# The pair of token blocks: products that pile up in one PSUM bank, weight sums on GpSimd, weight splits one f-tile ahead

## The chip, the cores and the metric

The kernel runs on one core of a Trainium2 chip. The metric is the device time of one execution in microseconds (us). The kernel before took 931.39 to 933.38 us in three runs, median 931.68.

Engines are named as the profile names them: PE is TensorE (its matmuls), PEld its weight loads, DVE is VectorE, ACT is ScalarE, POOL is GpSimd, SP issues DMAs. PSUM has eight banks, of which one 128x384 or 128x512 fp32 tile fills one. In the names of the profile "arena" and "arena_r" are the two views of the kernel's large SBUF buffer (float32 and fp32r), "ov_..." are buffers that take turns in one SBUF region, "banks" is PSUM, and "x2d" is a scratch tensor in DRAM.

## The reference

Three layers, one after the other, over 2304 tokens (4 batches of 576) of width 512:

```
x = linear attention(q, k, v)                      # features exp(+-(x@w_phi - max)), 8 heads of 64
g = x @ moe_w_gate                                 # 512 -> 1536
y = (g * sigmoid(g) * (x @ moe_w_val)) @ moe_w_out # 1536 -> 512
e = argmax(y @ moe2_w_gate)                        # 8 experts, one per token
out = prob[e] * sigmoid((y @ moe2_w_output_gate)[e]) * (relu(y @ w1[e]) @ w2[e])
```

The change lies in the second layer, the gated feed-forward.

## The kernel before, in words

Every fp32 product of the feed-forward is made of three fp32r matmuls: an operand is split in a high part (an ACT copy that rounds to fp32r, L549) and a low part (what is left, a subtraction on POOL, L552), and high·high, high·low and low·high are added up in PSUM. A weight tile is 128x512 for a block alone.

The tokens are cut in six blocks of 384 (n = 0 to 5), the width 1536 in twelve f-tiles of 128. Blocks 0 to 3 go one by one: for each f the gate product, the value product, the gate in between, and the output product of the f-tile before (`mm_o`). Blocks 4 and 5 go together, as "the pair" (L670). There the four products of a 2x2 block matrix are made of seven half products (Strassen and Winograd): A11, A12 and A22 are blocks of the weights, S1 to S4 sums of blocks, and the other operand is a block of x or one of the sums that `x_sums` has made of it (L638). In the order of the code a half product is six matmuls of 128x384 (L665 to L667), an output product nine of 128x512 (L619 to L621). So an f-tile of the pair has 42 + 9 matmuls on PE.

Each half product's weights are 256 wide and pass through a ring of 2048 columns (`ring`, `ahead`): as soon as a product is issued, what now has room is split. Before the first piece of an f-tile, `sums` makes the four weight sums on DVE (L558 to L561).

The products A11 to A22 of an f-tile land in four banks BA, BB, BX, BY. What they give is joined on DVE, ACT and POOL through SBUF: u2 is A11 (an ACT copy, L679) plus S2; z is S1 (ACT, L683) plus S3 (ACT, L686; the addition is on POOL); GP is the gate of A11+A12 (tanh L689, L690); gb is the gate of u2 plus S4 (L694, L695); va is GP times (u2 plus A22), which is split by L699 and one more addition for block 4's output product; and HB5, kept for later, is gb times (u2 plus z). The additions all go through `add` (L673), and its `eng` says where.

`rest` (L1226) puts in the output product of f-1 at the end of an f-tile, and steps of the third layer's routing (`fill`) in between: short DVE, ACT and PE work on the tokens that are ready. After the pair, the output product of block 4's last f-tile, its transposes and writes to x2d follow, and then block 5's twelve output products (L1247), each of HB5 split by `h5`. The first expert weights (`load_w`, `mw`) are fetched meanwhile.

The order on each engine is that of the program as a scheduler has sorted it per engine; what an instruction waits for are the tiles that it reads and writes, and each engine takes its instructions in order.

Of the kernel before, what the change touches and what calls it, by code (L numbers as in the profile page):

```python
# [23 lines left out]
NFT = DFF // P  # L24
# [157 lines left out]
def kernel(ctx, tc, qT, kT, v1, wphi, w1cat, wlog, mw1, mw2, consts, out):  # L182
# [334 lines left out]
    PRODS = ("A11", "S2", "S1", "S3", "A12", "S4", "A22")  # L517
    for f in range(NFT):
        uses += [(4, f, w) for w in PRODS] + [(4, f - 1, 2) if f else (3, NFT - 1, 2)]
    uses.append((4, NFT - 1, 2))  # L520
    uses += [(5, f, 2) for f in range(NFT)]
    where = {u: i for i, u in enumerate(uses)}
    ring, at_ = [], 0
    for u in uses:
        w = 512 if u[2] in (0, 1, 2) else 256
        if at_ % 2048 + w > 2048:
            at_ += 2048 - at_ % 2048
        ring.append((at_, w))
        at_ += w

    def wh(i):
        o, w = ring[i]
        return AR[:, 9216 + o % 2048:9216 + o % 2048 + w]

    def wl(i):
        o, w = ring[i]
        return AR[:, 11264 + o % 2048:11264 + o % 2048 + w]

    def source(i):
        n, f, w = uses[i]  # L540
        if w in (0, 1, 2):
            return WR[f][w]
        if w[0] == "A":
            o = 256 * (int(w[2]) - 1)
            return WR[f][int(w[1]) - 1][:, o:o + 256]
        return SS[f % 2][int(w[1]) - 1]

    def split_hi(i):
        ACT.activation(wh(i), source(i), AF.Copy)  # L549

    def split_lo(i):
        POOL.tensor_tensor(out=wl(i), in0=source(i), in1=wh(i).bitcast(F32), op=ALU.subtract)  # L552

    def sums(f):
        g0, g1 = WR[f][0][:, 0:256], WR[f][0][:, 256:512]
        v0, v1 = WR[f][1][:, 0:256], WR[f][1][:, 256:512]
        s1, s2, s3, s4 = SS[f % 2]
        DVE.tensor_tensor(out=s1, in0=v0, in1=v1, op=ALU.add)  # L558
        DVE.tensor_tensor(out=s2, in0=s1, in1=g0, op=ALU.subtract)
        DVE.tensor_tensor(out=s3, in0=g0, in1=v0, op=ALU.subtract)  # L560
        DVE.tensor_tensor(out=s4, in0=g1, in1=s2, op=ALU.subtract)  # L561

    def ahead(i):
        j = state["split"]
        while j < len(uses) and ring[j][0] + ring[j][1] - ring[i][0] <= 2048:
            if uses[j][2] == "A11":
                sums(uses[j][1])
            split_hi(j)
            split_lo(j)
            j += 1  # L570
# [748 lines left out]
```

## Time and profile before

| what | value |
|---|---|
| median of three runs | 931.68 us |
| the profiled execution | 931.75 us, of which 930.0 is the span on the core |
| PE busy | 888.2 us (96%) |
| DVE, ACT, POOL busy | 650.9, 573.3, 425.9 us (70, 62, 46%) |
| the pair, 490.3 to 622 us | 131.7 us, granted clock 0.99 |
| block 5's output products | to about 660 us |

A busy share is of the span. Matmuls are pipelined: each row gives a modelled duration of 0.33 us for a 128x384 matmul, but the next one starts earlier than that, so what a stretch costs PE is read from one start to the next, and a wait from a start that comes late. The granted clock is 1.00 where the engine runs at 2.4 GHz, and about 0.5 where it runs at 1.2 GHz. Rows of waits say which instruction of which line an engine stood idle for.

### The profile page before, as it was taken

The page shows a single profiled execution, that of the slowest core. Times are in us where ns is not written, and L with a number is a line of the kernel's source. Part 1 is how long each engine was busy: PE and PEld are TensorE (multiplying, and loading weights), DVE is VectorE, ACT ScalarE, POOL GpSimd, SP SyncE. Part 2 cuts the span into 40 slices and gives each one's busy share as a digit, 9 for nine tenths or more (in the row PEclk, how much of TensorE's full clock was granted, in tenths as well). Part 3 has the DMA queues.
Part 4 walks back from the last instruction along what each step waited for, and adds up shares of the span by engine and source line. Part 5 has one row for each costly group of instructions (what it writes and reads, how often), then busy time and mean ns, then how long its engine had stood idle before and what let it go on. Part 6 is the DMA issues. An engine that isn't in the chain of part 4 may idle for free. (4 is left out here: it accounts for less than half of the span.)

```text
span 930.0 us, 18143 instructions
## 1 busy us (share of the span) xinstructions
PE 888.2 (96%) x6979; PEld 769.6 (83%) x6979; DVE 650.9 (70%) x1075; ACT 573.3 (62%) x1051; POOL 425.9 (46%) x371
## 2 busy tenths in 40 slices
PE   8899999999999999999999988888999999999995
PEld 6789999999988899888888878776787888888884
DVE  6998785444337334554666889755799988899984
ACT  6877776444454444444545454445488988988883
POOL 1668988455543343335376676675104111222200
PEclk9999999999999999999999999998999999999998
DMA  8867542200111011200000000008401147156150
GB/s 242 222 179 205 188 141 63 75 1 1 27 50 27 15 41 29 72 16 1 2 1 35 1 1 2 1 11 314 151 24 35 47 132 279 71 186 260 44 191 9
DMA packets 20940, 78.88 MB, mean 85 GB/s; under 512 B 5359, under 2 KB 5615, under 8 KB 19057
## 3 DMA queue, kind: packets, MB, share of 16 engines
q1 hardware_dynamic: 17280, 67.60, 22.7%
q0 software_dynamic: 3200, 9.48, 3.1%
q8 instruction: 56, 0.92, 0.4%
q10 hardware_dynamic: 368, 0.60, 0.2%
q14 instruction: 36, 0.29, 0.1%
HBM read 123.24 MB, written 10.00 MB: 143 GB/s over the span
## 5 line engine op out<-in xcount | busy, mean ns | idle before, releaser
L552 POOL TENSOR_TENSOR arena_r<-arena,arena_r 128x512 fp32r<-128x512 f32 (+1 forms) x252 | 287.7, 1155 | 236.0 <-ACT arena_r L549 232.6
L549 ACT ACTIVATE arena_r<-arena 128x512 fp32r<-128x512 f32 (+1 forms) x252 | 137.7, 556 | 160.1 <-PE banks L581 94.0
L1052 DVE TENSOR_TENSOR arena_r<-arena,arena_r 128x1024 fp32r<-128x1024 f32 x160 | 188.0, 1224 | 20.7 <-ACT arena_r L1049 19.8
L1049 ACT ACTIVATE arena_r<-arena 128x1024 fp32r<-128x1024 f32 x160 | 161.2, 1066 | 15.9 <-PE banks L1088 10.2
L580 PE MATMUL banks<-arena_r 128*128 128x384 f32 x384 | 135.3, 352 | 2.3 <-DVE arena L592 1.7
L582 PE MATMUL banks<-arena_r 128*128 128x384 f32 x384 | 129.0, 336 | 0.0
L581 PE MATMUL banks<-arena_r 128*128 128x384 f32 x384 | 128.9, 336 | 0.0
L1088 PE MATMUL banks<-arena_r 128*128 128x512 f32 x480 | 116.2, 396 | 0.1
L1116 POOL DMA_INDIRECT out_dram<-arena x20 | 21.7, 1084 | 203.0 <-ACT arena L1115 202.7
L1088 PEld LDWEIGHTS banks<-arena_r 128*128 128x128 f32 x480 | 88.3, 188 | 19.9 <-ACT arena_r L1080 1.7
L619 PE MATMUL banks<-arena_r 128*128 128x512 f32 x216 | 88.1, 408 | 3.6 <-ACT arena_r L699 3.6
L621 PE MATMUL banks<-arena_r 128*128 128x512 f32 x216 | 86.5, 403 | 1.1 <-DVE arena_r L673 1.1
L620 PE MATMUL banks<-arena_r 128*128 128x512 f32 x216 | 86.3, 399 | 0.0
L580 PEld LDWEIGHTS banks<-arena_r 128*128 128x128 f32 x384 | 72.1, 188 | 7.8 <-DVE arena L592 2.1
L592 DVE SCALAR_TENSOR_TENSOR arena<-arena,banks 128x384 f32<-128x384 f32 x48 | 26.5, 551 | 70.7 <-ACT arena L589 70.7
L581 PEld LDWEIGHTS banks<-arena_r 128*128 128x128 f32 x384 | 72.3, 188 | 0.6
L582 PEld LDWEIGHTS banks<-arena_r 128*128 128x128 f32 x384 | 72.1, 188 | 0.0
L1110 PE MATMUL banks<-arena_r 128*128 128x512 f32 x160 | 62.6, 391 | 1.0 <-ACT arena_r L1049 0.7
L1112 PE MATMUL banks<-arena_r 128*128 128x512 f32 x160 | 62.6, 391 | 0.0
L1111 PE MATMUL banks<-arena_r 128*128 128x512 f32 x160 | 62.5, 390 | 0.0
L320 DVE TENSOR_REDUCE arena<-banks 128x6 f32<-128x768 f32 x48 | 45.8, 954 | 22.4 <-PE banks L312 21.5
L312 PEld LDWEIGHTS banks<-arena 64*128 64x128 f32 x576 | 39.5, 187 | 17.2 <-issue 7.1
(160 smaller groups left out, 1745.1 us busy)
## 6 DMA issues: line engine op xcount, KB each, us to landing
arena<-mw SPq DMA_DIRECT2D x40, 2048.0 KB
ov_conv<-w1cat SPq DMA_DIRECT2D x24, 512.0 KB
arena<-w1cat SPq DMA_DIRECT2D x12, 512.0 KB
arena<-v SPq DMA_DIRECT2D x16, 325.0 KB
x2d<-arena SPq DMA_DIRECT2D x18, 256.0 KB
arena<-qT SPq DMA_DIRECT2D x15, 288.0 KB
arena<-kT SPq DMA_DIRECT2D x15, 288.0 KB
arena<-consts ACTq DMA_DIRECT2D x1, 327.5 KB
```

Source lines behind the costliest of these rows:

```text
L549: ACT.activation(wh(i), source(i), AF.Copy)
L552: POOL.tensor_tensor(out=wl(i), in0=source(i), in1=wh(i).bitcast(F32), op=ALU.subtract)
L580: PE.matmul(ps, w_h[:, c], xh, start=(k == 0), stop=False)
L581: PE.matmul(ps, w_h[:, c], xl, start=False, stop=False)
L582: state["pe"] = PE.matmul(ps, w_l[:, c], xh, start=False, stop=(k == 3)).ins
L619: PE.matmul(ps, gh[:, ts_], woh, start=(f == 0), stop=False)
L620: PE.matmul(ps, gh[:, ts_], wol, start=False, stop=False)
L621: PE.matmul(ps, gl[:, ts_], woh, start=False, stop=(f == NFT - 1))
L1049: a = ACT.activation(h, src, AF.Copy)
L1052: DVE.tensor_tensor(out=l, in0=src, in1=h.bitcast(F32), op=ALU.subtract)
L1088: PE.matmul(PS[:, HB[h], :], lhs, w[:, h * 512:(h + 1) * 512], start=a, stop=b)
L1110: PE.matmul(ps, HTH[:, k, :], wh[:, cs], start=(k == 0), stop=False)
```

## The change

All 12 f-tiles of the pair are written anew:

- A11, S2, S1 and S4 are added up in one bank `bb` (bank 3 or 6 in turn), and ACT copies what stands there three times on the way: `sp1` after A11, `su2` after S2, `su4` after S1. A12 goes to bank 4 alone, S3 and then A22 to bank 5. What was joined through SBUF is joined by DVE with one operand and the result in PSUM. The POOL addition is gone.
- The order of the products is A11, A12, S2, S3, S1, S4, A22 (it was A11, S2, S1, S3, A12, S4, A22). The output product of f-1 is cut in two: two token tiles between S1 and S4, one after A22.
- The weights pass through four fixed slots of 512 columns. A11|A12, S1|S2 and S3|S4 are split as pairs; A22 has a place of its own, and the output weights too (`W2`). The low parts of S1|S2 and S3|S4 are made on DVE (L639), the others on POOL. The four sums move from DVE to POOL (L656). All splits of an f-tile are issued in the f-tile before.
- `x_sums` works in PSUM: no POOL additions, ACT puts two blocks there and DVE adds and subtracts in place.
- After the pair, the first two loads of expert weights are issued ahead of block 4's transposes; block 5's f-tiles 0 and 1 run ahead of block 4's last output product; the routing steps start at f = 2 there. Bank numbers of later parts change, the four memsets of the gather buffer move from POOL to DVE, and blocks 2 and 3 spread the attention steps by other limits (`need`, `span`).

```diff
-    def add(out_, x, y, op=ALU.add, eng=DVE):
-        eng.tensor_tensor(out=out_, in0=x, in1=y, op=op)
...
-            product(f, "A11", BA, True)
-            ACT.activation(u2, pa, AF.Copy)
-            product(f, "S2", BB, True)
-            add(u2, u2, pb)
-            product(f, "S1", BX, True)
-            ACT.activation(z, px, AF.Copy)
-            rest(f, 0)
-            product(f, "S3", BY, True)
-            ACT.activation(s7, py, AF.Copy)
-            add(z, z, s7, eng=POOL)
-            product(f, "A12", BA, False)
...
-            product(f, "S4", BX, False)
-            add(gb, u2, px)
...
-            product(f, "A22", BY, False)
-            add(va, u2, py)
-            add(va, GP, va, ALU.mult)
-            ACT.activation(GH[f % 2], va, AF.Copy)
-            add(GL[f % 2], va, GH[f % 2].bitcast(F32), ALU.subtract)
-            rest(f, 2)
-            add(z, u2, z)
-            add(HB5[f], gb, z, ALU.mult)
+    def cut(w, src, eng):
+        ACT.activation(w[0], src, AF.Copy)
+        eng.tensor_tensor(out=w[1], in0=src, in1=w[0].bitcast(F32), op=ALU.subtract)
...
+    def pair_split(i):
...
+        if w == 0:
...
+            cut(slot(i), WR[f][0], POOL)
+            for o, x, y, op in ((s1, v0, v1, ALU.add), (s2, s1, g0, ALU.subtract), (s3, g0, v0, ALU.subtract),
+                                (s4, g1, s2, ALU.subtract)):
+                POOL.tensor_tensor(out=o, in0=x, in1=y, op=op)
+        else:
+            cut(slot(i), SPR[f % 2][w - 1], DVE)
...
+        def gate(out_, ps):
+            ACT.activation(TS, ps, AF.Tanh, scale=0.5)
+            DVE.scalar_tensor_tensor(out=out_, in0=TS, scalar=1.0, in1=ps, op0=ALU.add, op1=ALU.mult)
...
+        def hidden(f):
+            if f >= 0:
+                copy(GH[f % 2], py)
+                add(GL[f % 2], py, GH[f % 2].bitcast(F32), ALU.subtract)
...
+            product(f, "A11", bb, True)
+            copy(sp1, pb)
+            hidden(f - 1)
+            product(f, "A12", BA, True)
+            add(pa, sp1, pa)
+            product(f, "S2", bb, False)
+            copy(su2, pb)
+            gate(GP, pa)
+            pair_split(3 * f + 3)
+            product(f, "S3", BY, True)
+            rest(f, 0)
+            product(f, "S1", bb, False)
+            copy(su4, pb)
+            pair_split(3 * f + 4)
+            add(pa, su4, py)
+            o_part(f, (0, 1))
+            rest(f, 1)
+            product(f, "S4", bb, False)
+            gate(gb, pb)
+            pair_split(3 * f + 5)
+            product(f, "A22", BY, False)
+            add(HB5[f], gb, pa, ALU.mult)
+            add(py, su2, py)
+            add(py, GP, py, ALU.mult)
+            cut22(f + 1)
+            o_part(f, (2,))
+            cut(W2, WR[f][2], POOL)
+            rest(f, 2)
+            if f == NFT - 1:
+                h5(0)
+                h5(1)
+        hidden(NFT - 1)
...
-    h5(0)
-    mm_o(4, NFT - 1)
-    for i in range(3):
-        post_x2(4, i)
+    pair(rest)
     fill(100)
-    state["banks"] = [1, 2, 4]
-    todo += post(4)
     load_w(0, 0)
     load_w(0, 1)
-    rows()
...
+        if f == 1:
+            o_tiles(4, NFT - 1, range(3), OUTB, (GH[1], GL[1]), W2)
+            for i in range(3):
+                post_x2(4, i)
+            rows()
```

DVE in an f-tile of the pair, before (a late tile, in which no routing step stands; earlier tiles have the four sums L558 to L561 besides). L673 is `add`, L690 the gate GP, L695 the gate gb:

```order
L673 TENSOR_TENSOR arena<-arena,banks 128x384
L673 TENSOR_TENSOR arena<-arena 128x384
L690 SCALAR_TENSOR_TENSOR arena<-arena,banks 128x384
L673 TENSOR_TENSOR arena<-arena,banks 128x384 x2
L695 SCALAR_TENSOR_TENSOR arena<-arena 128x384
L673 TENSOR_TENSOR arena<-arena 128x384 x2
L673 TENSOR_TENSOR arena_r<-arena,arena_r 128x384
```

The same in the changed program. L692 is now `add`, L699 both gates (GP first), L639 the low part of a pair of weight sums:

```order
L692 TENSOR_TENSOR arena_r<-banks,arena_r 128x384
L692 TENSOR_TENSOR banks<-arena,banks 128x384
L639 TENSOR_TENSOR arena_r<-arena,arena_r 128x512
L699 SCALAR_TENSOR_TENSOR arena<-arena,banks 128x384
L639 TENSOR_TENSOR arena_r<-arena,arena_r 128x512
L692 TENSOR_TENSOR banks<-arena,banks 128x384
L699 SCALAR_TENSOR_TENSOR arena<-arena,banks 128x384
L692 TENSOR_TENSOR banks<-arena,banks 128x384
L692 TENSOR_TENSOR arena<-arena,banks 128x384
L692 TENSOR_TENSOR banks<-arena,banks 128x384
```

The rows begin with block 4's low part there, which before ended the tile. The additions of u2 and z ahead of the gate GP are gone, the low parts of two weight pairs stand among the joins, and all six `add` rows have an operand in PSUM, four of them their result too.

ACT in an f-tile before. L549 are the weights' high parts, L679, L683 and L686 the copies, L689 and L694 the tanh of GP and gb, L699 the high part of block 4's hidden values:

```order
L679 ACTIVATE arena<-banks 128x384
L549 ACTIVATE arena_r<-arena 128x512
L549 ACTIVATE arena_r<-arena 128x256
L683 ACTIVATE arena<-banks 128x384
L549 ACTIVATE arena_r<-arena 128x256
L686 ACTIVATE arena<-banks 128x384
L549 ACTIVATE arena_r<-arena 128x256
L689 ACTIVATE arena<-banks 128x384
L549 ACTIVATE arena_r<-arena 128x256
L694 ACTIVATE arena<-arena 128x384
L549 ACTIVATE arena_r<-arena 128x256
L699 ACTIVATE arena_r<-arena 128x384
```

The same in the changed program: L695 are the copies (to arena_r: block 4's hidden values), L698 the tanh, L638 the high parts:

```order
L695 ACTIVATE arena<-banks 128x384
L695 ACTIVATE arena_r<-banks 128x384
L638 ACTIVATE arena_r<-arena 128x512
L698 ACTIVATE arena<-banks 128x384
L695 ACTIVATE arena<-banks 128x384
L638 ACTIVATE arena_r<-arena 128x512
L695 ACTIVATE arena<-banks 128x384
L638 ACTIVATE arena_r<-arena 128x512
L698 ACTIVATE arena<-banks 128x384
L638 ACTIVATE ov_pair<-arena 128x256
L638 ACTIVATE arena_r<-arena 128x512
```

A high part of 512 columns now stands between the hidden values' copy and the tanh of GP, and another ahead of the tanh of gb. Block 4's hidden values are split behind the copy sp1 of the next f-tile.

Routing steps on DVE before, from block 4's low part of one f-tile to the gate GP of the next. L832 and L840 are the routing's element-wise and reducing helpers:

```order
L958 CAST arena<-arena 128x5
L832 TENSOR_TENSOR arena<-arena 128x3
L840 TENSOR_REDUCE arena<-arena 128x12
L961 CAST arena<-arena 128x3
L832 TENSOR_TENSOR arena<-arena 128x96
L832 TENSOR_TENSOR arena<-arena 128x12
L840 TENSOR_REDUCE arena<-arena 128x12
L673 TENSOR_TENSOR arena<-arena,banks 128x384
L558 TENSOR_TENSOR arena<-arena 128x256
L559 TENSOR_TENSOR arena<-arena 128x256
L673 TENSOR_TENSOR arena<-arena 128x384
L690 SCALAR_TENSOR_TENSOR arena<-arena,banks 128x384
```

The same steps in the changed program (L873 and L881 are those helpers, L998 and L999 the former L957 and L958), from the addition of su4 to the gate gb of f-tile 5:

```order
L873 TENSOR_TENSOR arena<-arena 128x40
L881 TENSOR_REDUCE arena<-arena 128x5
L998 TENSOR_SCALAR arena<-arena 128x5
L873 TENSOR_TENSOR arena<-arena 128x96
L999 CAST arena<-arena 128x5
L873 TENSOR_TENSOR arena<-arena 128x3
L881 TENSOR_REDUCE arena<-arena 128x12
L1002 CAST arena<-arena 128x3
L873 TENSOR_TENSOR arena<-arena 128x96
L873 TENSOR_TENSOR arena<-arena 128x12
L881 TENSOR_REDUCE arena<-arena 128x12
L699 SCALAR_TENSOR_TENSOR arena<-arena,banks 128x384
```

The routing steps stood ahead of the joins that lead to GP, and now stand ahead of gb. The f-tiles 3 and 5 have 18 such rows each, f-tile 4 has 7, and f-tile 7 has 5.

## Rows read from the trace of the kernel before

**Rows 1.** The page's first part: busy us, share of the span, instructions of each engine.

```profile
PE 888.2 (96%) x6979; PEld 769.6 (83%) x6979; DVE 650.9 (70%) x1075; ACT 573.3 (62%) x1051; POOL 425.9 (46%) x371
```

**Rows 2.** Windows: us, busy (x instructions) by engine, PEclk, DMA share, GB/s.

```profile
490.30:622.00 131.70, 120.53 (x645) 108.53 (x646) 102.71 (x195) 65.48 (x168) 90.99 (x104) 0.99 0.02 7
523.00:535.00 12.00, 11.51 (x62) 9.96 (x60) 11.86 (x32) 5.42 (x16) 7.24 (x9) 1.00 0.00 0
571.00:574.40 3.40, 3.40 (x12) 3.40 (x12) 3.40 (x8) 1.78 (x5) 0.90 (x2) 0.51 0.02 5
612.00:622.00 10.00, 9.63 (x51) 8.57 (x50) 5.62 (x9) 4.85 (x11) 7.29 (x10) 1.00 0.01 2
629.10:636.00 6.90, 5.84 (x14) 4.05 (x14) 2.80 (x4) 2.76 (x6) 5.26 (x5) 0.51 0.71 228
```

**Rows 3.** Waits of PE, 480 to 670: us in total, times, longest.

```profile
PE banks L665 <- DVE arena L690: 9.8, 10, 1.9
PE banks L619 <- ACT arena_r L699: 3.6, 1, 3.6
...
PE banks L621 <- DVE arena_r L673: 1.1, 1, 1.1
```

**Rows 4.** Timeline of PE, 534.5 to 537: start, us, instruction, [idle before <-releaser].

```profile
534.59 0.40 PE L620 MATMUL banks<-arena_r 128*128 128x512 f32 x1
534.83 0.40 PE L621 MATMUL banks<-arena_r 128*128 128x512 f32 x1
535.64 0.45 PE L665 MATMUL banks<-arena_r 128*128 128x384 f32 x1 [0.42 <-DVE arena L690]
535.92 0.34 PE L666 MATMUL banks<-arena_r 128*128 128x384 f32 x1
...
536.97 0.33 PE L666 MATMUL banks<-arena_r 128*128 128x384 f32 x1
```

**Rows 5.** Timeline of DVE and PE, 544 to 548.

```profile
544.33 1.22 DVE L558 TENSOR_TENSOR arena<-arena 128x256 f32<-128x256 f32 x1 [0.63 <-POOL arena_r L552]
...
546.43 1.00 DVE L673 TENSOR_TENSOR arena<-arena 128x384 f32<-128x384 f32 x1
547.35 0.54 DVE L690 SCALAR_TENSOR_TENSOR arena<-arena,banks 128x384 f32<-128x384 f32 x1
...
547.95 0.45 PE L665 MATMUL banks<-arena_r 128*128 128x384 f32 x1 [1.94 <-DVE arena L690]
```

**Rows 6.** Timeline of DVE at 624.

```profile
624.15 0.56 DVE L673 TENSOR_TENSOR arena<-arena 128x384 f32<-128x384 f32 x1 [4.33 <-POOL arena L673]
```

**Rows 7.** Groups of DVE, 490.3 to 622: busy us, mean ns, idle before <-releasers.

```profile
L673 DVE TENSOR_TENSOR arena<-arena 128x384 f32<-128x384 f32 x33 | 25.7, 806 | 11.3 <-POOL arena L673 11.3
L673 DVE TENSOR_TENSOR arena<-arena,banks 128x384 f32<-128x384 f32 x34 | 18.3, 544 | 6.0 <-ACT arena L679 4.5 <-PE banks L667 1.5
L832 DVE TENSOR_TENSOR arena<-arena 128x24 f32<-128x24 f32 (+12 forms) x21 | 9.8, 476 | 0.2
L558 DVE TENSOR_TENSOR arena<-arena 128x256 f32<-128x256 f32 x9 | 9.7, 1075 | 7.9 <-POOL arena_r L552 7.8
...
L673 DVE TENSOR_TENSOR arena_r<-arena,arena_r 128x384 fp32r<-128x384 f32 x11 | 6.0, 548 | 0.3
```

**Rows 8.** Groups of POOL by shape, 503 to 622.

```profile
L552 POOL TENSOR_TENSOR arena_r<-arena,arena_r 128x256 fp32r<-128x256 f32 x72 | 59.4, 843 | 37.9 <-ACT arena_r L549 37.9
L552 POOL TENSOR_TENSOR arena_r<-arena,arena_r 128x512 fp32r<-128x512 f32 x12 | 15.9, 1329 | 0.0
```

**Rows 9.** Groups of ACT by shape, 503 to 622.

```profile
L549 ACT ACTIVATE arena_r<-arena 128x512 fp32r<-128x512 f32 x13 | 8.0, 618 | 0.0
...
L694 ACT ACTIVATE arena<-arena 128x384 f32<-128x384 f32 x10 | 5.3, 526 | 38.1 <-DVE arena L673 38.1
L683 ACT ACTIVATE arena<-banks 128x384 f32<-128x384 f32 x11 | 5.2, 476 | 0.0
```

**Rows 10.** Timeline of DVE at 643.

```profile
643.40 0.69 DVE L854 COPY arena<-banks 128x512 f32<-128x512 f32 x1 [3.25 <-DMA x2d<-arena]
```

More of the change, by code (lines that the diff above doesn't have):

```diff
@@ L563, in ahead, with split_hi @@
[L563 to L570, printed above, removed]
-        state["split"] = j
+    where = {u: i for i, u in enumerate(uses)}
+    def split_hi(i):
+        n, f, w = uses[i]
+        ACT.activation(WH[i % 4], WR[f][w], AF.Copy)
+    def split_lo(i):
+        n, f, w = uses[i]
+        POOL.tensor_tensor(out=WL[i % 4], in0=WR[f][w], in1=WH[i % 4].bitcast(F32), op=ALU.subtract)
@@ L610, in act_v, with o_tiles @@
         g_lo(f)
[L612 to L617 removed]
+    def o_tiles(n, f, ts, out_, g, w):
+        (gh, gl), (woh, wol) = g, w
+        for t in ts:
+            ps = PS[:, out_[t], :]
             ts_ = slice(t * P, (t + 1) * P)
@@ L659, in product @@
-    def product(f, name, bank_, start):
-        i = where[4, f, name]
-        ps, w_h, w_l = PS[:, bank_, :BT], wh(i), wl(i)
-        xh, xl = OPX[name]
+        t3 = [t[:, i * 768:i * 768 + 768] for i in range(3)] + [AR[:, 14848:15616]]
+        t3 = [x.rearrange("p (k t) -> p k t", k=2) for x in t3]
+        opx.update(A11=XHL[0, 0], A12=XHL[1, 0], S4=XHL[1, 1], S3=XHL[0, 1], S1=t3[0:2], S2=t3[2:4],
+                   A22=(XH[:, 0, 0:2, :], XL[:, 0, 0:2, :]))
+        opx["w22"] = (t[:, 2304:2560], AR[:, 15616:15872])
@@ L663, in product @@
+    PLACE = {"A11": (0, 0), "A12": (0, 1), "S1": (1, 0), "S2": (1, 1), "S3": (2, 0), "S4": (2, 1)}
+    def product(f, name, bank_, start):
+        if name == "A22":
+            w = opx["w22"]
+        else:
+            j, h = PLACE[name]
+            w = [x[:, h * 256:h * 256 + 256] for x in slot(3 * f + j)]
+        ps = PS[:, bank_, :BT]
+        xh, xl = opx[name]
         for k in range(2):
             c = slice(k * P, (k + 1) * P)
-            PE.matmul(ps, w_h[:, c], xh[:, k, :], start=(start and k == 0), stop=False, skip_group_check=True)
@@ L705, in h5, with cut22 @@
+            PE.matmul(ps, w[0][:, c], xh[:, k, :], start=(start and k == 0), stop=False, skip_group_check=True)
+            PE.matmul(ps, w[0][:, c], xl[:, k, :], start=False, stop=False, skip_group_check=True)
+            state["pe"] = PE.matmul(ps, w[1][:, c], xh[:, k, :], start=False, stop=(k == 1), skip_group_check=True).ins
+    def cut22(f):
+        if f < NFT:
+            cut(opx["w22"], WR[f][1][:, 256:512], POOL)
     def h5(f):
         if f < NFT:
-            ACT.activation(GH[f % 2], HB5[f], AF.Copy)
```

203 lines of the change are left out of this document (99 added, 104 removed).

## The prediction

> **What bounds the kernel now.** I read the busy shares first. PE is busy for 888.2 of 930.0 us and no other engine comes near [rows 1], so the change can only pay where PE stands still. The windows come next: in the pair PE is busy for 120.53 of 131.70 us although its clock is at 0.99, while DVE stands at 102.71 and POOL at 90.99 [rows 2]. PE's waits then say for whom it waits: ten times, 9.8 us in all, a half product stands for DVE's L690, the gate GP [rows 3]. GP reads bank BA, in which A11 of the next f-tile is to start. Behind the pair the first output product of block 4's last f-tile stands 3.6 us for ACT's L699, and a later matmul of it 1.1 us for DVE's low part.
>
> The timeline shows why GP is late. At 544.33 DVE begins a weight sum, 0.63 us late because POOL had not read the old sums, and two further steps later GP starts at 547.35, PE 0.60 us after that [rows 5]. The groups name the price of these steps: an addition with both operands in SBUF takes 806 ns, the same shape with one in PSUM 544; a 256-wide sum takes 1075 [rows 7]. So DVE's queue ahead of GP is the limit, not its total load: the stretch without sums and routing has 5.62 us of DVE in 10.00, the one with both 11.86 in 12.00 [rows 2]. The end of the pair has another cause of the same sort: DVE's addition into HB5 stood 4.33 us for POOL's sum z [rows 6], and block 4's hidden values are queued behind it.
>
> A wait costs more than its idle time. The last 128x512 matmul before one starts at 534.83, the next 128x384 at 535.64, the one behind it 0.28 later [rows 4]. Undisturbed, the steps are 0.24 (534.59 to 534.83) and (536.97 - 535.92) / 6 = 0.175. Lost are 0.81 + 0.28 - 0.24 - 0.175 = 0.68 us for a shown idle time of 0.42, so 0.27 beyond what is shown.
>
> **What the change removes.** PE's own work stays 42 + 9 matmuls per f-tile. A11 no longer lands in the bank that GP reads, so the ten waits for L690 go; at the end of the pair there is no POOL addition, and block 4's hidden values are made from PSUM in two steps while two f-tiles of block 5 run ahead of them, so 3.6 and 1.1 go too. These 12 waits are 9.8 + 3.6 + 1.1 = 14.5 shown and 12 x 0.27 = 3.2 beyond: 17.7 us. With two of these waits went a lower clock: 0.51 from 571.0 to 574.4, with 12 matmuls of 128x384 in 3.40 us instead of 12 x 0.175 = 2.1, and 0.51 from 629.1 to 636.0, with 14 of 128x512, which want 14 x 0.24 = 3.4 of 6.9, less the 1.1 + 0.27 of the wait counted above [rows 2, 3]. These are 1.3 and 2.1: 3.4 us, if no long wait follows elsewhere (0 if one does each time). Removed: 21.1 us.
>
> **What it adds in an f-tile without routing.** The longest chain leads from S4's fifth matmul (which frees the slot for the next high part) to S1 of the next f-tile. By the order of the instructions: high part of 512 (0.62), tanh (0.53), gate gb, py + su2, HB5, py times GP on DVE (four of 0.54), ACT's copy of the hidden values (0.48), their low part and the addition of sp1 (0.55, 0.54), tanh (0.53), the copy su2 (0.48) [rows 7, 9]. That is 0.62 + 0.53 + 2.16 + 0.48 + 1.09 + 0.53 + 0.48 = 5.89. The first step starts about 0.4 behind the matmul (it ends 0.33 after its start), and six changes of engine cost some 0.04 each, as from L690's end at 547.89 to PE's start at 547.95 [rows 5]: 6.5 us. PE gets there after two matmuls of S4, A22, three output matmuls, A11, A12, S2 and S3: 32 x 0.175 + 3 x 0.24 = 6.3, of which 0.1 is the step that a released matmul pays later anyway: 6.2. It lacks 0.3, nothing if neighbours on DVE overlap by 0.07 as they mostly do. I take 0.25 for 11 borders of f-tiles: 2.8 us, with bounds of 0 and 0.6 each (6.6). A12 stands in this chain for HB5, which reads its bank: most of the loss would be booked there.
>
> The three copies are each on the path. S2 waits for sp1: 0.33 + 0.05 + 0.48 + 0.06 = 0.92 from A11's last matmul, while A12 fills 7 x 0.175 - 0.1 = 1.12. It is hidden by 0.2. S4 waits for su4, which stands behind a high part of 512 that waits for S1's fifth matmul: 0.4 + 0.62 + 0.48 + 0.06 = 1.56, against one matmul of 0.175 and six of 0.24, less 0.1, which is 1.5. It is about even, and inside the bounds above. If the cover is gone each of the three costs its idle time and 0.27.
>
> The load per f-tile is no bound. DVE has eight instructions of 0.54 and two low parts of 512, which the trace has not on DVE: between 0.55 (its 384-wide low part) and 1.33 (POOL's for 512) [rows 7, 8]; the DVE row is nearer in kind and gives 0.55 x 512 / 384 = 0.73. That is 5.8 of some 9.4 us. POOL has two cuts of 512, one of 256 and four sums: 2 x 1.33 + 5 x 0.84 = 6.9 [rows 8].
>
> **Routing steps.** In the changed order DVE's stretch from GP to the gate gb has room. GP ends 0.5 us behind a tanh that ends about 0.3 before S1 wants su2, and gb can start 4.5 us later; less the low part and one addition (1.27) this leaves 3.2. F-tiles 3 and 5 put 18 routing instructions there, f-tile 4 seven and f-tile 7 five. At the mean of 476 ns of the element-wise ones [rows 7], and half that for most others, 18 are 6 to 7.6 us, so 2.8 to 4.4 late; less what they gain from beginning earlier, since some stand ready while PE waits. I take 2.0, 0.3, 2.8 and 1.0: 6.1 us, between 1 (they fit, as the fall of DVE's load allows) and 13. The cost is before A12 again, through gb and HB5. A wait of 3 us may bring the lower clock with it; one such stretch of 1.3 at even odds is 0.7.
>
> The Trainium skill's page SBUF — State Buffer, section "Who interferes with whom", says that a DVE instruction with two SBUF inputs contends with a GpSimd instruction that reads SBUF, and that the second one fully blocks until the first ends, while with one SBUF input it does not. By that rule, the trace agrees: 806 against 544 ns for the same shape [rows 7]. It speaks for the joins in PSUM and against the sums on POOL, which now lie beside the routing steps and the low parts; the first rival below says what that would make.
>
> **Other edits.** Block 4's x2d writes stand in the queue behind two loads of expert weights instead of one; DVE's copy L854 already waits 3.25 us for such a write [rows 10], and more of it can reach PE's transposes: 0.5, between 0 and 2. `x_sums` has more DVE work (14 instructions of 768 instead of 8) but in blocks where DVE has time, the pacing of the attention steps, the bank numbers and the memsets move no work on PE: 0, between -1 and 2 together.
>
> **Sum.** Added: 2.8 + 6.1 + 0.7 + 0.5 = 10.1. The profiled execution took 931.75 us (0.07 above the median of 931.68): 931.75 - 21.1 + 10.1 = 920.8 us. For this case alone, 914 to 925.
>
> **Rivals.**
> First: the routing steps become what PE waits for. For it: DVE is at 11.86 of 12.00 where they stand now [rows 2], and the loaded POOL does not get lighter. Then the late 4.4 us fall in full on f-tiles 3 and 5, 1.5 on the two others together, and two stretches of the lower clock come: 10.3 + 2.6 instead of 6.1 + 0.7 gives 926.9. Against it: no sums stand in between any more. The page rule above would act through this case.
>
> Second, slower than before: the accumulation in one bank. Each f-tile has three places where PE cannot go on before ACT has copied the bank. For it: ACT takes its instructions in order, and 512-wide high parts that wait for PE stand ahead of su4 and the tanh of gb; su4's margin is nothing. If each of 36 copies comes late by a shown 0.4, it costs 36 x 0.67 = 24.1 in place of 2.8: 942.1. It decides from about 0.38 each, 36 x 0.65 = 23.4, where all that was gained is gone. Against it: sp1 has 0.2 to spare and ACT is busy for half of the pair (65.48 of 131.70).
>
> Third, no change: the waits only move. If HB5 and su2 are late by as much as GP was, 11 waits of 1.0 + 0.27 and the clock's 3.4 come back: 14.0 + 3.4 - 2.8 on top, 935.4 at worst, and 931.7 if the clock stays up.
>
> Fourth, better: the chains are as short as the overlaps allow, and the routing steps fit: 931.75 - 21.1 + 1 + 0.5 = 912.2, or 911 if the other edits give their one microsecond too.
>
> **Chances.** A measurement of this kernel tells about 0.2% (1.9 us) from no change. The forecast has 0.52, the first rival 0.17, the second 0.09, the third 0.08 (half of it within 0.2%, half above), the fourth 0.14. Faster: 0.52 + 0.17 + 0.14 = 0.83; same 0.04; slower 0.09 + 0.04 = 0.13. The range goes from 910.0, nearly the fourth's end, to 929.0, just past the first rival; what is left out are the second and the third, 0.17 together.
>
> **What would show it.** Right: no wait of a half product for the gate GP, none of 3.6 us behind the pair, f-tiles without routing some 9.4 to 9.7 us apart, waits of A12 for HB5 in f-tiles 4 and 6, just behind those with 18 routing steps, of 1.5 to 3 us, DVE's additions near 0.54. Wrong: waits for the copies sp1, su2 or su4 in every f-tile (second rival), low parts on DVE of over 1.2 us, or a stretch at half clock behind each routing f-tile. A loss outside the pair and block 5 would be outside this working altogether.

## The result, and the profile after

The changed kernel takes 905.59 us (median of four runs, 905.05 to 907.5) against 931.86 before: 0.9719 of it, interval 0.9701 to 0.9737. That is 26.3 us less, where 11.0 were forecast, and under the lower end of the range. The profiled execution took 905.5 us with a span of 903.7.

The page's first part answers to [rows 1]: PE's busy time hardly changes, since its work is the same.

```profile
PE 880.8 (97%) x6979; PEld 766.8 (85%) x6979; DVE 622.9 (69%) x1049; ACT 576.1 (64%) x1017; POOL 391.0 (43%) x339
```

The time lies where PE stood still. Three starts on PE mark the stretches: the first and the last matmul of the half products, and the last output matmul of block 5. Before, they started at 490.30, 622.35 and 666.59.

```profile
485.91 0.33 PE L672 MATMUL banks<-arena_r 128*128 128x384 f32 x1
...
606.54 0.33 PE L674 MATMUL banks<-arena_r 128*128 128x384 f32 x1
...
639.88 0.39 PE L580 MATMUL banks<-arena_r 128*128 128x512 f32 x1
```

| stretch | before | after | difference | forecast |
|---|---|---|---|---|
| up to the pair | 490.30 | 485.91 | -4.4 | 0 |
| the pair's half products | 132.05 | 120.63 | -11.4 (-12.8) | -4.2 |
| from there to block 5's end | 44.24 | 33.34 | -10.9 (-9.5) | -6.8 |
| the rest of the span | 263.4 | 263.8 | +0.4 | 0 |

In brackets is the difference after six output matmuls (6 x 0.23 = 1.4 us) are put back in their stretch: the new order has moved them ahead of the pair's last product. The forecast column splits the prediction's own sum.

The windows (columns as in [rows 2]): the pair, and the stretch behind.

```profile
486.00:606.50 120.50, 117.30 (x654) 109.16 (x653) 79.89 (x172) 66.94 (x137) 67.88 (x76) 1.00 0.02 8
606.50:640.00 33.50, 31.83 (x159) 25.04 (x158) 24.82 (x53) 18.95 (x34) 17.94 (x14) 1.00 0.83 307
```

In the pair DVE fell from 102.71 of 131.70 us to 79.89 of 120.50 and POOL from 90.99 to 67.88. The clock is at 1.00 throughout; both stretches at half clock are gone. The waits of PE, where [rows 3] had 9.8, 3.6 and 1.1 us:

```profile
PE banks L672 <- DVE arena L692: 2.7, 1, 2.7
PE banks L894 <- DVE arena L895: 1.5, 1, 1.5
PE banks L672 <- DVE arena_r L562: 0.4, 1, 0.4
```

No product waits for a gate any more. One wait of 2.7 us for HB5 (an L692) is left in the pair, and 1.5 us for the transposes of block 4 behind it.

A late f-tile shows what became of the forecast's chain from S4 to S1, first on ACT, then on DVE, then on PE. S4's fifth matmul starts at 585.80.

```profile
586.17 0.63 ACT L638 ACTIVATE arena_r<-arena 128x512 fp32r<-128x512 f32 x1 [1.42 <-PE banks L673]
...
589.14 0.49 ACT L695 ACTIVATE arena<-banks 128x384 f32<-128x384 f32 x1 [0.37 <-PE banks L674]
589.53 0.48 ACT L695 ACTIVATE arena_r<-banks 128x384 fp32r<-128x384 f32 x1
...
591.56 0.49 ACT L695 ACTIVATE arena<-banks 128x384 f32<-128x384 f32 x1
```

```profile
588.15 0.55 DVE L692 TENSOR_TENSOR arena<-arena,banks 128x384 f32<-128x384 f32 x1
588.61 0.55 DVE L692 TENSOR_TENSOR banks<-arena,banks 128x384 f32<-128x384 f32 x1
590.05 0.56 DVE L692 TENSOR_TENSOR arena_r<-banks,arena_r 128x384 fp32r<-128x384 f32 x1 [0.88 <-ACT arena_r L695]
```

```profile
588.77 0.33 PE L674 MATMUL banks<-arena_r 128*128 128x384 f32 x1
588.95 0.33 PE L672 MATMUL banks<-arena_r 128*128 128x384 f32 x1
...
592.10 0.44 PE L672 MATMUL banks<-ov_pair,arena_r 128*128 128x384 f32 x1
```

The high part (L638) starts at 586.17, the tanh at 586.71, the gate gb at 587.21, HB5 at 588.15 and A12 on PE at 588.95, 0.25 us behind HB5's end: no wait. The last join (times GP) ends at 589.16. The hidden values are copied only at 589.53, behind the copy sp1 in ACT's queue, and sp1 (589.14) had waited for A11's last matmul, which starts at 588.77. So the forecast's long chain has some 0.4 us to spare here. What S1 waits for is a shorter chain that begins at A11's end: sp1, the hidden values (589.53, low part 590.05), sp1 into A12 (590.52), the tanh of GP (591.17), su2 (591.56 to 592.05), S1 at 592.10. From A11's last matmul that is 3.33 us, where PE's 19 steps of 0.173 ask for 3.29. With the longer first step behind it (0.28 instead of 0.175) about 0.15 us is lost per f-tile.

The forecast's 6.5 us had been added up from durations, but on both engines the next instruction starts before the one ahead ends (the tanh 0.54 behind a high part of 0.63, DVE every 0.47 at 0.55 each).

### The profile page after: what moved, and what is told of

Read it like the earlier page. It is cut to its first block, busy times and chain, and to the rows that moved or that the text cites. A ratio compares the mean times of both kernels' runs of the same rounds, so it can differ in the third digit from the quotient of the medians.

```text
span 903.7 us, 17926 instructions
## 1 busy us (share of the span) xinstructions
PE 880.8 (97%) x6979; PEld 766.8 (85%) x6979; DVE 622.9 (69%) x1049; ACT 576.1 (64%) x1017; POOL 391.0 (43%) x339
## 5 line engine op out<-in xcount | busy, mean ns | idle before, releaser
L525 POOL TENSOR_TENSOR arena_r<-arena,arena_r 128x512 fp32r<-128x512 f32 x143 | 184.0, 1291 | 175.5 <-ACT arena_r L521 175.3
L521 ACT ACTIVATE arena_r<-arena 128x512 fp32r<-128x512 f32 x143 | 90.1, 631 | 157.7 <-PE banks L542 98.2
L638 ACT ACTIVATE arena_r<-arena 128x512 fp32r<-128x512 f32 (+1 forms) x73 | 43.8, 613 | 51.0 <-PE banks L673 32.4
```

What stands on the lines that cost most here:

```text
L521: ACT.activation(WH[i % 4], WR[f][w], AF.Copy)
L525: POOL.tensor_tensor(out=WL[i % 4], in0=WR[f][w], in1=WH[i % 4].bitcast(F32), op=ALU.subtract)
```

## The experiments

Most runs change one thing, a few put such edits together. "Before" in a ratio is the kernel before on the same chip in the same set; its median lay between 931.9 and 935.3, so ratios are compared across sets, and 0.001 is 0.9 us.

**Was it the bank, or DVE's load?** Two edits of the kernel before, one of the changed kernel.

```
b_s2_first:   PRODS = ("S2", "A11", "S1", ...); product S2 ahead of A11
b_sums_pool:  -    DVE.tensor_tensor(out=s1, ...)  (s1 to s4)
              +    POOL.tensor_tensor(out=s1, ...)
a_sums_dve:   -    POOL.tensor_tensor(out=o, in0=x, in1=y, op=op)
              +    DVE.tensor_tensor(out=o, in0=x, in1=y, op=op)
```

> The kernel before, with S2 ahead of A11 in every f-tile, so that the bank which the gate GP reads is started on six matmuls (1.05 us) later. Theory A (the pair was slow because a bank's next product waited for a gate at the end of DVE's queue): the waits for L690, 9.8 us shown, lose up to 1.05 each, so some 3 us of them stay and about 7 to 8 us are gained: 923 to 925. Theory B (DVE's load was the cause, and a later bank only moves the wait to the next join): no gain, 930 to 932, with new waits for DVE elsewhere in the f-tile.

> The kernel before, with the four weight sums on POOL and nothing else changed. Theory B (the load on DVE): DVE's queue ahead of GP loses 2.7 us per f-tile, the waits for L690 fall under 2 us in all, and most of the pair's gain comes with this alone: 918 to 923. Theory A (the banks and the joins): POOL had 90.99 of 131.70 us in the pair and gets 40 x 0.84 = 33 more, so the sum z and the low parts on POOL come late in its queue and PE waits for these instead: 928 to 938.

> The changed kernel, with the four weight sums back on DVE. Theory A: no product waits for a gate that stands directly behind the sums, DVE has room in the f-tiles without routing, and only the f-tiles with 18 routing steps get some 1 to 2 us later each: 906 to 909. Theory B: DVE's queue is again the limit, 2.7 us per f-tile on the joins, and 8 us or more come back: 913 to 920.

b_s2_first: 936.17 us, 1.0028 (1.0018 to 1.0038): no gain, so theory A as stated here fails. Theory B had no gain too, but with new waits for DVE; the new ones name ACT. Its waits of PE, and two rows of its ACT:

```profile
PE banks L665 <- ACT arena L680: 9.8, 11, 1.4
...
PE banks L665 <- DVE arena L690: 1.9, 5, 0.5
```

```profile
541.57 0.53 ACT L699 ACTIVATE arena_r<-arena 128x384 fp32r<-128x384 f32 x1 [1.57 <-DVE arena L673]
...
543.13 0.47 ACT L680 ACTIVATE arena<-banks 128x384 f32<-128x384 f32 x1
```

The waits for GP fell from 9.8 to 1.9, and 9.8 us of waits for ACT's copy of A11 (L680 there) took their place. That copy is queued on ACT behind the hidden values L699, which start at 541.57 when DVE is through with its joins, and behind three high parts of weights. The wait only changed its name.

b_sums_pool: 936.76 us, 1.0037 (1.0022 to 1.0051). Moving the sums off DVE alone gains nothing. PE's waits for GP grow, and DVE itself now stands for POOL's sum z (its waits in the pair, behind PE's):

```profile
PE banks L665 <- DVE arena L690: 11.7, 10, 1.7
```

```profile
DVE arena L673 <- POOL arena L673: 32.7, 10, 6.3
```

In its pair of 135.1 us DVE is down to 91.7 us of work and POOL up to 123.4. So the run does not tell what a lighter DVE would be worth by itself: the load went to the engine that DVE waits for.

a_sums_dve: 905.8 us, 0.9694 (0.968 to 0.9709), not slower than the changed kernel. The sums' engine is not what was won. This is against theory B. In its trace the pair is 1.9 us shorter (the wait of 2.7 us is 0.8) and the stretch behind it 1.7 us longer.

**One chain over three queues.**

```
b_z_dve:      -    add(z, z, s7, eng=POOL)          +  add(z, z, s7)
b_s2_hidden:  b_s2_first, and hidden(f - 1) (high and low part of va)
              tied behind ACT's copy of A11 of f
b_chain:      both of these together
b_chain_pool: b_chain, and the four sums on POOL
```

> The kernel before, with the addition of S1 and S3 (z) on DVE instead of POOL, and nothing else. If the 3.6 us wait behind the pair comes from z in POOL's queue, that wait falls under 0.5 us, the 1.1 us behind it and the stretch at half clock go with it: 6 to 7 us less there. DVE gets 12 additions of 0.8 us but loses 11.3 us of idle time on POOL, so the waits for L690 change by less than 3 us either way: 922 to 929 in all. Rival (the end of the pair is a chain on DVE and ACT and POOL only the last name in it): the 3.6 us wait stays above 2.5 us, and the total is 930 to 936.

> The kernel before with S2 ahead of A11, and with the high part of block 4's hidden values tied behind ACT's copy of A11 of the next f-tile (and its low part behind the addition of S2). Theory E (the pair was slow because one chain runs through both engines' queues: what PE waits for stands behind the hidden values of the f-tile before, on DVE or on ACT): the 9.8 us of waits for the copy of A11, which S2 ahead of A11 had brought, go as well, and 6 to 10 us are gained on the kernel before: 922 to 927. Rival (DVE's and POOL's work itself does not fit in an f-tile): the waits move to a third place, less than 2 us are gained, 930 or more.

> The kernel before with three of its orders changed and its SBUF joins, sums on DVE and ring kept: z on DVE, S2 ahead of A11, and block 4's hidden values tied behind ACT's copy of the next A11. Theory E (one chain over the queues of DVE, ACT and POOL made the pair slow): the pair falls from 132 to 121 to 125 us, and the kernel to 919 to 924. Rival (each of these waits only hides the next, and it is the joins with PSUM operands, 544 instead of 806 ns, that shorten an f-tile): the pair stays at 126 us or more, as with z alone, and the kernel at 926 to 930.

> The three reorderings of the kernel before together (z on DVE, S2 ahead of A11, hidden values behind the next copy of A11), with the four weight sums on POOL as well. If DVE's load is what is left (9.2 of 9.4 us in its best f-tiles): DVE falls to about 6.5, the pair to 121 to 122.5 us and the kernel to 920 to 922. If POOL cannot take them: POOL had 7.6 to 8.4 us per f-tile there and gets 3.4 more, over the 9.4 of PE, so the pair goes back to 128 us or more and the kernel to 926 to 932.

b_z_dve: 928.68 us, 0.9943 (0.9922 to 0.9965). POOL's one addition was worth some 5 us, with DVE's work increased:

```profile
PE banks L665 <- DVE arena L690: 6.2, 6, 1.6
...
PE banks L619 <- ACT arena_r L699: 1.3, 1, 1.3
```

The wait for L699 fell from 3.6 to 1.3, short of the expected 0.5, and the gain lies in the pair (126.6 us instead of 132.05), where the waits for GP fell by 3.6 us, more than the expectation allowed for. Behind it a wait for L854 grew from 1.2 to 2.5.

b_s2_hidden: 932.52 us, 0.9988 (0.9975 to 1.0): by its expectation the rival's outcome. The 9.8 us for the copy are gone from its waits and the pair is 129.0 us long, but the end of the pair now waits 4.1 us for the hidden values (3.6 before), and others behind it grew.

b_chain: 923.87 us, 0.988 (0.9865 to 0.9895), theory E's outcome. Three reorderings give 11 us, and the pair 124.2 us. Its windows show what is next:

```profile
492.00:616.00 124.00, 116.28 (x644) 107.46 (x645) 114.58 (x209) 66.86 (x168) 92.53 (x94) 1.00 0.02 8
568.30:577.70 9.40, 9.40 (x53) 8.93 (x52) 9.33 (x14) 5.46 (x14) 7.60 (x8) 1.00 0.00 2
577.70:588.90 11.20, 10.08 (x65) 9.21 (x64) 9.75 (x21) 5.35 (x14) 7.64 (x9) 1.00 0.00 1
```

```profile
PE banks L665 <- DVE arena L701: 2.5, 3, 1.1
```

Where DVE has 9.33 us of work in 9.40 an f-tile runs at PE's pace; with 9.75 and a late join it takes 11.2. b_chain_pool: 924.72 us, 0.9905 (0.9884 to 0.9927), between its two ranges (the pair took 125.4 us), with the second one's mechanism:

```profile
492.00:616.00 124.00, 118.11 (x641) 106.20 (x640) 103.23 (x169) 68.49 (x167) 120.22 (x135) 1.00 0.02 8
```

```profile
PE banks L667 <- POOL arena_r L552: 4.2, 10, 0.7
```

POOL is full, and the products wait for low parts. So the sums fit on neither engine as long as POOL makes the low parts of eight splits per f-tile and DVE the joins in SBUF. The changed kernel takes work from both at once: four wide splits and a narrow one instead of eight, no z, joins with PSUM operands. Which of these counts most was not separated: the other 4.9 us of the pair's 12.8, beyond b_chain's 7.9, have no run of their own.

**The margins of the new chain.**

```
a_su2_twice:   +   copy(su2, pb)        (a second time)
a_sbuf_joins:  -   add(py, su2, py); add(py, GP, py, ALU.mult)
               +   add(va, su2, py); add(va, GP, va, ALU.mult)   # SBUF; hidden() reads va
```

> The changed kernel, with ACT's copy su2 made twice, so that S1 can start one copy later (0.39 us from start to start on ACT). If the chain through the gate gb, HB5, the hidden values and su2 is as long as an f-tile of PE, as the trace of the changed kernel has it (S1 starts 0.05 us after the copy's end), each f-tile gets 0.35 to 0.5 us longer, 11 of them 4 to 6 us: 909.5 to 911.5. If the chain has slack, as a pair without any wait for su2 would suggest, less than 1 us: 905 to 906.5.

> The changed kernel with the two joins behind A22 (su2 + A22, times GP) written to SBUF instead of back to PSUM, and block 4's hidden values split from there: per f-tile one product and one low part have both operands in SBUF. If PSUM operands are what made the joins short: each of the two takes 0.8 us or more instead of 0.55, the chain to S1 gets 0.3 to 0.5 us longer per f-tile and PE follows it, 3 to 6 us in all: 909 to 912. If the order of the chain is what counts: under 1.5 us, 905.5 to 907.5.

a_su2_twice: 907.48 us, 0.9725 (0.9706 to 0.9743), between the two expectations; its pair took 122.3 us instead of 120.6. It is not a clean test, for the scheduler changed PE's order as well. From f-tile 5 on, two output matmuls stand ahead of S1 (one in f-tiles 0, 3 and 4), where the changed kernel has none:

```profile
593.19 0.40 PE L579 MATMUL banks<-arena_r 128*128 128x512 f32 x1
593.74 0.44 PE L672 MATMUL banks<-ov_pair,arena_r 128*128 128x384 f32 x1 [0.16 <-ACT arena L695]
```

These two steps of 0.23 us cover a copy of 0.39, and S1 still waits in places. That fits a chain without slack, but what the copy costs in the old order was not measured.

a_sbuf_joins: 907.24 us, 0.9707 (0.9689 to 0.9724), no difference in the total, against the first expectation. Six of the twelve f-tiles do get 0.25 to 0.29 us longer, 1.6 us in all, by slower instructions:

```profile
L692 DVE TENSOR_TENSOR arena_r<-arena,arena_r 128x384 fp32r<-128x384 f32 x11 | 8.3, 757 | 7.5 <-ACT arena_r L695 7.5
L692 DVE TENSOR_TENSOR arena<-arena 128x384 f32<-128x384 f32 x11 | 7.3, 665 | 0.0
```

against 0.55 us with PSUM. The 2.7 us wait fell to 1.7 in the same trace, which hides most of it.

**Ahead of the pair.**

```
a_xs_sbuf:  -  TSL = [PSF[:, o:o + 768] ... for o in (2560, 3328)]
            +  TSL = [A[:, kr + o:kr + o + 768] ... for o in (5120, 5888)]
```

> The changed kernel, with the x sums built up in SBUF instead of in PSUM; the same instructions in the same order. Theory C (the 4.4 us that block 3 gained come from the x sums' operand in PSUM): each of the 14 DVE steps of 768 columns takes 1.5 us or more instead of about 0.95, the gates of block 3 queue behind them again, and 3 to 5 us come back: 908.5 to 910.5. Rival D (they come from the attention steps being spread otherwise): within 1 us of the changed kernel, 905 to 906.5.

910.05 us, 0.9736 (0.972 to 0.9751), and 4.2 above a_sums_dve in the same set, of which 1.2 is that run's shorter pair: theory C. The group of DVE's additions of the x sums, before (L651), changed, and in this run:

```profile
L651 DVE TENSOR_TENSOR arena<-arena 128x768 f32<-128x768 f32 x4 | 6.0, 1494 | 3.0 <-POOL arena L648 3.0
```

```profile
L620 DVE TENSOR_TENSOR banks<-banks,arena_r 128x768 f32<-128x768 f32 x8 | 7.7, 960 | 0.5 <-ACT banks L616 0.4
```

```profile
L620 DVE TENSOR_TENSOR arena<-arena,arena_r 128x768 f32<-128x768 f32 x8 | 11.4, 1440 | 3.1 <-PE banks L542 3.1
```

```profile
PE banks L541 <- DVE arena_r L562: 1.7, 2, 1.2
```

With both operands in SBUF a 768-wide step takes 1.44 us instead of 0.96, block 3's low part L562 queues behind it, and the pair starts at 489.8: 3.1 us later than in a_sums_dve of the same set, 3.9 later than in the changed kernel's profile. Not all of the 4.4 us is the operand, though. The kernel before has a wait in block 3 that a_xs_sbuf does not bring back:

```profile
439.55 0.96 DVE L651 TENSOR_TENSOR arena<-arena 128x768 f32<-128x768 f32 x1 [1.33 <-POOL arena L648]
```

```profile
441.44 0.93 PE L312 MATMUL banks<-arena 64*128 64x128 f32 x6 [1.54 <-DVE arena L323]
```

There an x sum (L651) stood for POOL's addition L648, and an attention step (L323) behind it in DVE's queue. That addition is gone in a_xs_sbuf as well. (Of its own waits one is new, 1.1 us of an attention product for DVE.) What the other pacing of the attention steps gives was not tested by itself.

**Behind the pair.**

```
a_o4_first:    block 4's last output product, post_x2 and rows() in front of block 5's loop
a_o4_tied:     the same, and block 5's first matmul tied behind that product
a_loads_late:  load_w(0, 0), load_w(0, 1) tied behind block 4's x2d writes
a_best:        a_loads_late and a_sums_dve
a_no_tie6:     -  if f == 6: state["pe"] = mm.ins
```

> The changed kernel, with block 4's last output product, its transposes and the gather buffer ahead of block 5's f-tiles 0 and 1 again, as before. If the gain behind the pair (9.5 us of standing time less) came from running these two f-tiles ahead, the wait of 3 us or more for the hidden values and the stretch at half clock come back: 910 to 914. If it came from hidden values that are ready early (no POOL addition, the joins in PSUM), a wait of about 1 us appears, or none: 905 to 907.5.

> The changed kernel, with block 5's output products tied behind block 4's last one, so that none runs ahead of it. If running f-tiles ahead is what removed the 3.6 us wait: a wait of 1.2 to 2.5 us for ACT's copy or DVE's low part of the hidden values shows behind the pair, and 2 to 4 us are lost with the low clock that follows it: 907.5 to 910. If the hidden values are ready early by the shorter chain alone: under 1 us, 905 to 906.5.

> The changed kernel, with the first two loads of expert weights tied behind block 4's writes to x2d in SP's queue. If the wait of PE's transposes behind the pair (1.5 us for DVE's L895, which waits 3.24 us for a write of x2d) comes from these loads standing ahead in the queue, it goes: 903 to 904.5, with the loads done 3 to 5 us later and no wait for them at the third layer. If the loads' lateness is felt there, that takes the gain back: 905 to 908.

> The changed kernel with these loads behind the x2d writes and with the four weight sums on DVE, whose trace had a pair shorter by 1.9 us. If the two gains stand side by side: 901.5 to 903.5. If the one in the pair is again lost behind it: as the loads alone, 903.5 to 905.

> The changed kernel without the line that holds back the first three splits of expert weights until block 5's f-tile 6. If that holding back removed the 2.3 us wait for DVE's L883 (routing of block 4 behind 1024-wide low parts on DVE), a wait of 1.5 us or more for a routing step or for the transposes' copy comes back behind the pair: 907 to 909.5. If the wait went because the routing there starts two f-tiles later: within 1 us of the changed kernel.

a_o4_first (906.79 us, 0.9718, 0.9702 to 0.9735) left one f-tile of block 5 ahead by the scheduler's choice, and shows no wait for the hidden values. a_o4_tied (907.15, 0.9698, 0.9684 to 0.9711) shows none either, but it did not do what was meant: the tie holds only the first matmul of block 5, that of one token tile. Others ran ahead; this one starts while ACT's copy of the hidden values has not begun:

```profile
609.95 0.40 PE L583 MATMUL banks<-arena_r 128*128 128x512 f32 x1
```

```profile
610.05 0.49 ACT L699 ACTIVATE arena_r<-banks 128x384 fp32r<-128x384 f32 x1 [0.31 <-DVE banks L696]
```

So no run has block 5 really behind. In the changed kernel the copy ends at 609.22, while PE is done with the pair's output products at 607.40: without anything to run ahead, by these two times, some 1.8 us of wait would be left of the 3.6. One f-tile ahead (nine matmuls of 0.23 us) covers it; the second gives nothing more.

a_loads_late: 907.44, 0.9707 (0.9694 to 0.972), and the stretch behind the pair is 33.5 us long, with the loads early 33.3: the 1.5 us wait went and 1.7 us of waits for block 5's low parts came. a_best: 906.09, 0.9691 (0.9678 to 0.9704), by its ratio no better than a_sums_dve alone. a_no_tie6: 910.9, 0.974 (0.9725 to 0.9755), 3.2 above the changed kernel in the same set (a_ref) and above the range given:

```profile
PE banks L580 <- DVE arena_r L639: 3.4, 2, 2.1
```

Holding the first expert splits back keeps 1024-wide low parts out of block 5's way. The wait that returned is for block 5's own low parts, not for the routing step that was expected.

**The last wait in the pair, and the changed kernel once more.**

```
a_ref:     the changed kernel
a_spread:  route_early: empty steps between taken, experts, picks and place;
           first instruction of experts and of picks tied to the product at hand
```

> The changed kernel itself, as the measure for the others of this set: 904 to 908.

> The changed kernel, with three of the routing steps (the slots' experts and the two picks) held back and an empty step put in between, so that the 18 routing instructions of f-tile 5 lie as 7, 6 and 5 in f-tiles 5, 6 and 7 and the ones behind move on by one or two f-tiles. If the routing ahead of the gate gb is what makes A12 of f-tile 6 wait: the 2.7 us wait and the lower clock that follows it in some runs go, no other wait comes, since each piece fits the room of 3.2 us: 2.5 to 4.5 us less than the changed kernel, 0.966 to 0.969 of the kernel before. If the wait is another one with this name (the chain itself): as the changed kernel, 0.970 to 0.973.

a_ref: 907.72 us, 0.9712 (0.9696 to 0.9728). In its profile the f-tile with the 2.7 us wait took 13.98 us, in the changed kernel's 12.44: in this run the clock fell behind the wait.

```profile
550.92 0.66 PE L672 MATMUL banks<-arena_r 128*128 128x384 f32 x1 [2.75 <-DVE arena L692]
551.38 0.52 PE L673 MATMUL banks<-arena_r 128*128 128x384 f32 x1
551.70 0.52 PE L674 MATMUL banks<-arena_r 128*128 128x384 f32 x1
```

The steps are 0.32 us there instead of 0.175. a_spread: 903.19 us, 0.9687 (0.9663 to 0.971), the fastest of all; its interval overlaps that of the changed kernel in the other sets, its pair is 117.9 us instead of 120.6, and the wait for L692 is gone from the list:

```profile
PE banks L894 <- DVE arena L895: 1.9, 1, 1.9
```

## Why the prediction was wrong

The direction was right and so was the sum's largest term, the waits that went. The other terms were wrong, nearly all to the same side. Forecast was 11.0 us less, measured 26.3; the 15.3 us between them are 4.4 ahead of the pair, 8.6 in it, 2.7 behind it, and 0.4 the other way in the rest.

**Ahead of the pair (0 forecast, 4.4 measured).** "`x_sums` has more DVE work ... but in blocks where DVE has time ...: 0, between -1 and 2 together." This is the step that failed outright. Block 3's products wait there for DVE, behind the x sums, in rows that [rows 3] leaves out or that lie ahead of its window (1.7 us for L592, 1.5 for L323). The 1.5 us went with POOL's addition, and a_xs_sbuf loses 3.1 to 3.9 us by moving the operand to SBUF, so the operand's price of [rows 7] held for these steps as well.

**Routing in the pair (6.8 with the clock forecast, 2.9 measured).** "I take 2.0, 0.3, 2.8 and 1.0: 6.1 us". Only f-tile 5 cost anything: its routing fills DVE from 544.28 to the gate at 548.95, HB5 starts at 549.87, and A12 of the next f-tile waits.

```profile
548.95 0.54 DVE L699 SCALAR_TENSOR_TENSOR arena<-arena,banks 128x384 f32<-128x384 f32 x1
...
549.87 0.54 DVE L692 TENSOR_TENSOR arena<-arena,banks 128x384 f32<-128x384 f32 x1
```

```profile
547.39 0.34 PE L674 MATMUL banks<-arena_r 128*128 128x384 f32 x1
550.47 0.45 PE L672 MATMUL banks<-arena_r 128*128 128x384 f32 x1 [2.74 <-DVE arena L692]
```

Undisturbed, the second start would come 0.175 behind the first: 2.9 us are lost, forecast were 2.8. Behind f-tiles 3, 4 and 7 there is no wait. The mean of 476 ns does not describe either f-tile with 18 instructions: in f-tile 3 they took 3.4 us in all (522.02 to 523.65, 524.73 to 526.47), in f-tile 5 6.7 (541.22 to 543.21, 544.28 to 548.95), of the 6 to 7.6 forecast for both. So f-tile 5's hit is in part luck, for what made it long was not the number of instructions. A cast and the three instructions of these rows (the last row holds two) took four to eight times what they take elsewhere, beside low parts that POOL makes (DVE's rows first, then POOL's):

```profile
545.59 1.26 DVE L873 TENSOR_TENSOR arena<-arena 128x3 f32<-128x3 f32 x1
...
547.47 1.39 DVE L873 TENSOR_TENSOR arena<-arena 128x96 f32<-128x96 f32 x2
```

```profile
545.50 1.33 POOL L639 TENSOR_TENSOR arena_r<-arena,arena_r 128x512 fp32r<-128x512 f32 x1
...
547.48 1.36 POOL L639 TENSOR_TENSOR arena_r<-arena,arena_r 128x512 fp32r<-128x512 f32 x1
```

DVE's rows end within 0.03 us of POOL's. In a_sums_dve the same instructions are short:

```profile
547.55 0.15 DVE L873 TENSOR_TENSOR arena<-arena 128x3 f32<-128x3 f32 x1
...
549.71 0.33 DVE L873 TENSOR_TENSOR arena<-arena 128x96 f32<-128x96 f32 x2
```

There the first falls between two of POOL's low parts (546.25 to 547.61 and 547.57 to 548.30), the second behind the last of them (549.53). With the cast between them (0.62 against 0.16) it is 3.27 us against 0.64: the difference, 2.6 us, is nearly the whole wait. Another cast, long in a_sums_dve (1.27 us at 546.37), again ends with a low part of POOL's. a_spread makes the pieces smaller and takes them out of this place at once, so it shows that the wait comes from the routing ahead of gb, and not which of the two counts.

**The chain in the pair (2.8 forecast, some 1.6 measured).** "It lacks 0.3, nothing if neighbours on DVE overlap by 0.07 as they mostly do. I take 0.25 for 11 borders of f-tiles: 2.8 us". The long chain through gb and HB5 has some 0.4 us to spare; 0.15 us per f-tile comes from the shorter one that begins at sp1, and it falls on S1, not on A12. Durations were added where starts should have been subtracted.

Routing and chain leave about 3.5 of the pair's 8.6 us. The first f-tile's wait for DVE's low part L601 (1.1 us, now 0.4 for L562) and one of 0.2 for L686, which the sum leaves out, are about 1.1 of these; the rest is spread over small steps and not put down to anything.

**Behind the pair (6.8 forecast, 9.5 measured).** Of the 14.5 us of waits named as removed, all went. But the sum left out two waits as if they had to stay. The 2.3 us for L883 went too (0.2 is left, for L924), and a_no_tie6 shows that one line I had not priced is worth 3 us there. The 1.2 us for L854 did stay (now 1.5). Of the 3.6 us for the hidden values about half went because these are ready earlier, and half, by the estimate above, because block 5 runs ahead.

The mechanism behind the largest term was only half right: the cause of the waits for GP was only in part DVE's queue "ahead of GP": b_s2_first shows that another wait stood right behind, and b_chain that order and POOL's z were 7.9 of the pair's 12.8. The half clock did not return in this profile, but in a_ref, behind the wait that the forecast had put it behind.

Of its signs, three came: no wait for the gate GP, late f-tiles 9.55 us apart, and a wait of A12 for HB5 in f-tile 6; that in f-tile 4 did not. The first rival (routing becomes the bound) happened in one f-tile of four, and by the means that it named, POOL beside DVE. The second (the copies) did not: S2 started 0.36 us behind sp1's end (589.63 to 589.99). The third did not. The fourth, 911 to 912, was nearest and still too high by what happened outside the pair. Two of the rivals' sums are off, without touching the range: what the second needs to undo the gain is 13.8 us, 0.38 for each of 36 copies in all and not with 0.27 on top, and the third without the clock is 932.0.

The Trainium skill's rule on two SBUF inputs (SBUF — State Buffer, "Who interferes with whom") was weighed for the joins and against the sums. By that rule the x sums should have been priced too, and there the trace agrees: 1.44 against 0.96 us for 768 columns in the mean, and 0.95 in SBUF too for the one (468.49 in a_xs_sbuf) beside which POOL stood idle.

## What to carry to other kernels

When an engine waits for the last link of a chain that runs through the queues of three others, removing one link moves the wait; undo the order of the whole chain and the load of each queue together, and price every edit by the row of its own kind, also where no wait of the main engine points at it. Take a chain's length from start to start in one timeline, not from a sum of durations, and a step's price from its own shape and from what the engine beside it does at that moment. Where a run shows no effect, look in its trace whether the scheduler did what the edit meant. An instruction that is ready but not urgent, such as a first split of later weights, is better held back than left to stand ahead of a short one (3 us here).

## What the runs showed of the hardware

The clock's fall behind one and the same 2.7 us wait comes in some executions and not in others: the f-tile took 13.98 us in a_ref (granted clock 0.50 from 551 to 554 us) and 12.44 in the profile of the changed kernel (1.00 there), with the same program.

An addition on DVE with both operands in SBUF is not slow by itself. In the kernel before one of 128x384 took 0.55 us at 581.37, while POOL was idle, and one took 1.07 at 592.40, beside POOL's low parts. The 0.806 of [rows 7] is a mean of such rows.

The kernel before had medians of 931.9 to 935.3 us in six sets, and of 933.6 and 935.3 in two sets on the same chip: more than most single edits here are worth.
